# Splitting the last store of an MLP kernel over two queues and widening the zero constant of its opening matmuls

## The chip, the cores and the metric

The kernel runs on one core of one Trainium2 chip. The metric is the device time of one execution in microseconds; before the change it is 124.99 us, the median of three runs (124.86 to 125.08). Engines are named as in the profile: PE multiplies matrices (PEld is its loading of weights), DVE and ACT copy or transform tiles, POOL does small fills, SP only issues transfers. Transfers (DMAs) are issued by SP and by ACT, each on a queue of its own, and are carried out by 16 DMA engines that both queues share.

## The reference

```python
h = jnp.einsum("bsd,df->bsf", x, w1)      # x: 1 x 2048 x 640, w1: 640 x 1728
h = _silu(h)
out = jnp.einsum("bsf,fd->bsd", h, w2)    # w2: 1728 x 640, out: 1 x 2048 x 640
```

Everything is bf16 in memory: two matrix products with a SiLU between them.

## The kernel before

**Staging.** `x` comes in transposed by the DMA (`xT`, model dimension on the partitions), `w1` and `w2` lie in `w1s`, `w2s` and, for the last 64 rows of `w2`, `w2t`. The first product makes `hT`, the hidden dimension on the partitions, in groups of 512 tokens; ACT applies SiLU as it empties each PSUM bank. The second product makes the output. Columns 512 to 639 of the output are made transposed for 512 tokens at a time (class `Wide`), turned round by a DMA into `o_sb`; columns 0 to 511 are made token tile by token tile (class `Tok`), 128 tokens on the partitions. PSUM has eight banks of 512 columns; `bank()` hands them out in turn.

**The opening.** The program has a part that runs ahead of a barrier between the engines. `early` moves instructions into it. The order there: SP issues the transposing load of the first 512 tokens (two of the five blocks of `x`), ACT issues the first five column blocks of `w1`, DVE fills the small constant `z` with zero (line 125), and PE, as soon as `z` is filled, multiplies zero by zero: 13 dummy matmuls of 128 x 256 and then a pair of half width (lines 129 to 138). They write PSUM bank 3, which the first real matmul into it starts anew. Behind them on PE comes `opening()`: the real matmuls, which wait for the first `xT` and `w1s`. So a PE that starts its dummies later comes to its first real matmul later, unless the loads are later still. The two operands of a dummy are one column of `z`, repeated by a step of zero.

**The end.** The last four token tiles and a bit are not run in groups of four as the others, but one after the other: A, B, C (512 columns each), E (tile 15, columns 0 to 383) and G2 (tile 15, columns 384 to 511), lines 369 to 379. Each is closed by `close` (lines 314 to 325): an engine copies the bank into `o_sb`, then the tile is stored. E is copied by DVE and stored by SP; G2 is copied by ACT. Its store carries columns 384 to 639, that is G2's own 128 and the 128 turned ones: 128 rows of 512 bytes, 64 KB. It is the last store of the kernel, and the only one that ACT issues (`last` is true for it alone). At the end SP waits for all its stores and ACT for its one (lines 380 and 381):

```python
wait(sp, *stores)
wait(act, *stores_a)
```

No scheduler decides an order here: each engine's instructions stand in the order in which the code emits them, and semaphores (`wait`, `tick`) tie the engines together. Each DMA has a semaphore of its own, which rises as each of the 16 DMA engines reports.

Of the kernel before, what the change touches and what calls it, by code (L numbers as in the profile page):

```python
# [9 lines left out]
def bass_standalone__dense_activation_silu__prompt_kernel(  # L10
# [6 lines left out]
    bf16 = mybir.dt.bfloat16  # L17
# [3 lines left out]
    of = out.flatten_outer_dims()  # L21
    S, D = xf.shape
    F = w1.shape[1]
    P = 128
# [6 lines left out]
    HB = 256  # L31
# [7 lines left out]
    pe, act, dve, pool, sp = nc.tensor, nc.scalar, nc.vector, nc.gpsimd, nc.sync  # L39

    with ExitStack() as es:
        def sb(name, shape, dtype):
            return es.enter_context(nc.sbuf_tensor(name, shape, dtype))
# [7 lines left out]
        oT = sb("oT", [P, S], bf16)  # L51
        o_sb = sb("o_sb", [P, S // P, D], bf16)
        warm = sb("warm", [P, 32], fp32)
        z = sb("z", [P, 2], bf16)
        ps = es.enter_context(nc.psum_tensor("ps", [P, NB, BANK], fp32))

        count = {}
# [2 lines left out]
        def sem(name):  # L60
            s = es.enter_context(nc.semaphore(name))
            count[s.name if hasattr(s, "name") else name] = 0
            return [s, 0]

        def tick(ins, s, n=1):
            ins.then_inc(s[0], n)
            s[1] += n
            return (s, s[1])

        def wait(eng, *points):  # L70
            for pt in points:
                if pt is None:
                    continue
                s, v = pt
                key = (id(eng), id(s))
                if seen.get(key, 0) < v:
                    eng.wait_ge(s[0], v)
                    seen[key] = v
# [6 lines left out]
        def load(eng, out_ap, in_ap):  # L85
            s = sem(f"s_ld{n_dma[0]}")
            n_dma[0] += 1
            return tick(eng.dma_start(out=out_ap, in_=in_ap), s, 16)
# [40 lines left out]
        def dummies(n, w):  # L129
            for _ in range(n):  # L130
                for c0 in range(0, P, w):
                    pe.matmul(ps[c0:c0 + w, 3, 0:HB], lhsT=z[:, 0:1].broadcast_to([P, w]),  # L132
                              rhs=z[:, 0:1].broadcast_to([P, HB]), start=True, stop=True)

        def first_dummies():
            wait(pe, p_z)
            dummies(13, P)
            dummies(1, HC)
# [96 lines left out]
        for q in range(NSC // 2):  # L235
            b = bank()
            for k in range(DT):
                for hh in range(2):
# [3 lines left out]
                             start=(k == 0), stop=(k == DT - 1), shared=True)  # L242
# [4 lines left out]
        def evac(out_ap, in_ap, b, after, eng=None):  # L247
            e = eng or (dve, act)[evac_n[0] % 2]
            evac_n[0] += 1
            wait(e, after)  # L250
            if e is dve:
                r = tick(dve.tensor_copy(out=out_ap, in_=in_ap), s_dve)  # L252
            else:
                r = tick(act.copy(out=out_ap, in_=in_ap), s_act)  # L254
            bank_free[b] = r
            return r

        JB = SCH // P
        HP = P // 2
        stores, stores_a = [], []  # L260
        s_turn = [sem(f"s_turn{c}") for c in range(NSC)]
        st_w = [None] * NSC

        class Wide:
# [16 lines left out]
            def close(self, t):  # L281
                c = self.c
                r = evac(oT[:, c * SCH:(c + 1) * SCH], ps[:, self.b, :], self.b, t)
                wait(sp, r)
                st_w[c] = tick(sp.dma_start_transpose(
                    out=o_sb[:, c * JB:(c + 1) * JB, DA:D],
                    in_=oT[:, c * SCH:(c + 1) * SCH],
                ), s_turn[c], 16)

        class Tok:  # L290
# [23 lines left out]
            def close(self, t, eng=None):  # L314
                st, a, e = self.st, self.a, self.e
                r = evac(o_sb[:, st, a:e], ps[:, self.b, 0:e - a], self.b, t, eng)
                if e == DA:
                    e = D
                    last = a > 0
                else:  # L320
                    last = False
                q = act if last else sp
                wait(q, r, st_w[st // JB])
                (stores_a if last else stores).append(
                    load(q, of[st * P:(st + 1) * P, a:e], o_sb[:, st, a:e]))

        def lanes(up, down):
            for i in range(max(len(up), len(down))):
# [32 lines left out]
        last = None  # L361
        for q in range(NSC // 2):
            for j in range(0, JB, 2):
# [3 lines left out]
                else:  # L367
                    last = (s0, s1)
# [41 lines left out]
```

## Time and profile before

| | |
|---|---|
| median of three runs | 124.99 us (124.86 to 125.08) |
| profiled execution, its own time | 124.23 us |
| its span | 122.67 us |
| around the span | 1.56 us |
| PE busy | 120.2 us (98%), 1056 matmuls |
| ACT busy | 38.8 us |
| DVE busy | 6.8 us |
| last matmul starts / ACT's copy of G2 | 120.52 / 120.78 to 121.04 us |
| ACT's last store issued / landed / end of span | 121.07 / 122.63 / 122.67 us |

How to read it: the span runs from the first to the last instruction of the program on the core; a DMA issue is shown on its issuing engine as SPq or ACTq with the time that the issuing took, and the transfer itself goes on behind it. "Landing" is when the semaphore of a DMA is full. The profile is of one execution, which was 0.76 us shorter than the median of the runs, so differences are read from it and added to the median.

### The profile page before, as it was taken

To read this page: it belongs to the slowest core of one execution; us is meant where nothing else is said; L and a number is where in the kernel's file an instruction comes from. 1 tells how busy PE (TensorE), PEld (TensorE's weight loads), DVE (VectorE), ACT (ScalarE), POOL (GpSimd) and SP (SyncE) were. 2 spreads that over 40 slices of the span, in tenths; PEclk is the share of its full clock that TensorE was granted. 3 is DMA by queue.
4 is the path that set the end of the run, shared out by engine and by line. 5 is a ranking of instruction groups with operands and counts; after the bars stand their busy time and mean duration, and the time that the engine had idled before them with its cause. 6 is when DMAs were issued, how large, how long until landed. Compare 5 with 4: busy or idle time off the path is not lost.

```text
span 122.7 us, 2298 instructions
## 1 busy us (share of the span) xinstructions
PE 120.2 (98%) x1056; PEld 58.9 (48%) x1057; DVE 6.8 (6%) x11; ACT 38.8 (32%) x67; POOL 0.3 (0%) x5
## 2 busy tenths in 40 slices
PE   8999999999999999999999999999999999999993
PEld 5455545555555555555544444444444444444452
DVE  0000000000000000000000022002101200222001
ACT  0403975555555555555530011002101200110110
POOL 0000000000000000000000000000000000000000
PEclk9999999999999999999999999999999999999999
DMA  7999955455992000000000014202200220022122
GB/s 148 246 222 336 129 122 113 95 88 97 285 392 69 0 0 0 8 0 0 0 0 5 0 35 93 48 0 107 107 0 5 107 107 0 5 107 107 53 78 82
DMA packets 19481, 10.42 MB, mean 85 GB/s; under 512 B 13456, under 2 KB 18960, under 8 KB 19472
## 3 DMA queue, kind: packets, MB, share of 16 engines
q1 hardware_dynamic: 19184, 10.05, 32.0%
q10 hardware_dynamic: 288, 0.23, 0.7%
q8 instruction: 8, 0.13, 0.5%
q14 instruction: 1, 0.01, 0.0%
HBM read 4.51 MB, written 2.62 MB: 58 GB/s over the span
## 4 chain that ended last, share of the span: by engine, by line
PE 98%; issue 0%; ACT 0%; DVE 0%
PE ps L172 95%; PE ps L132 3%; ACT o_sb L254 0%; DVE z L125 0%
## 5 line engine op out<-in xcount | busy, mean ns | idle before, releaser
L172 PE MATMUL ps<-xT,w1s 128*64 128x512 bf16 x540 | 58.7, 380 | 0.0
L172 PE MATMUL ps<-w2s,hT 64*128 64x512 bf16 (+3 forms) x376 | 46.0, 369 | 0.2 <-issue 0.2
L172 PEld LDWEIGHTS ps<-xT,w1s 128*64 128x64 bf16 x540 | 30.0, 110 | 28.4 <-issue 0.2
L176 ACT ACTIVATE hT<-ps 128x512 bf16<-128x512 f32 x52 | 30.0, 607 | 24.5 <-PE ps L172 24.5
L172 PEld LDWEIGHTS ps<-w2s,hT 64*128 64x128 bf16 (+1 forms) x377 | 21.0, 95 | 24.1 <-issue 0.2
L254 ACT CAST o_sb<-ps 128x512 bf16<-128x512 f32 (+1 forms) x9 | 5.0, 551 | 41.5 <-PE ps L172 41.5
L172 PE MATMUL ps<-hT,w2s 64*128 64x512 bf16 x104 | 11.7, 376 | 0.0
L172 PEld LDWEIGHTS ps<-hT,w2s 64*128 64x128 bf16 x104 | 5.0, 94 | 6.3 <-issue 0.4
L252 DVE CAST o_sb<-ps 128x512 bf16<-128x512 f32 (+1 forms) x8 | 5.4, 675 | 40.5 <-PE ps L172 40.5
L252 DVE CAST oT<-ps 128x512 bf16<-128x512 f32 x2 | 1.4, 692 | 73.2 <-PE ps L172 73.2
L254 ACT CAST oT<-ps 128x512 bf16<-128x512 f32 x2 | 1.2, 586 | 10.6 <-PE ps L172 10.6
L132 PE MATMUL ps<-z 128*128 128x256 bf16 (+1 forms) x15 | 3.3, 419 | 0.4 <-DVE z L125 0.4
L172 PE MATMUL ps<-w2t,hTt 64*128 64x512 bf16 (+2 forms) x17 | 2.9, 363 | 0.0
L154 ACT ACT_TABLE_LOAD x1 | 1.3, 1283 | 4.7 <-DVEq L395 4.7
L132 PEld LDWEIGHTS ps<-z 128*128 128x128 bf16 (+1 forms) x15 | 1.9, 142 | 1.5 <-issue 0.4
L176 ACT ACTIVATE hTt<-ps 128x512 bf16<-128x512 f32 x2 | 1.2, 598 | 1.0 <-PE ps L172 1.0
L172 PEld LDWEIGHTS ps<-w2t,hTt 64*128 64x128 bf16 x17 | 0.9, 94 | 1.1
L172 PE MATMUL ps<-hTt,w2t 64*128 64x512 bf16 x4 | 0.8, 376 | 0.0
L172 PEld LDWEIGHTS ps<-hTt,w2t 64*128 64x128 bf16 x4 | 0.2, 94 | 0.2
L154 ACT ACTIVATE warm<-warm 128x32 f32<-128x32 f32 x1 | 0.2, 231 | 0.0
L141 POOL MEMSET warm<- 128x32 f32 x1 | 0.1, 124 | 4.3 <-POOLq L395 4.3
L395 POOL MEMSET const-bfloat16-1.0<- 128x1 bf16 x1 | 0.1, 101 | 0.0
(4 smaller groups left out, 0.4 us busy)
## 6 DMA issues: line engine op xcount, KB each, us to landing
out_dram<-o_sb SPq DMA_DIRECT2D x15, 160.0 KB, 1.8
w2s<-in_w_dram SPq DMA_DIRECT2D x1, 1120.0 KB, 6.3
w1s<-in_w_dram SPq DMA_DIRECT2D x4, 256.0 KB, 3.4
w2s<-in_w_dram SPq DMA_DIRECT2D x1, 960.0 KB, 8.5
w1s<-in_w_dram SPq DMA_DIRECT2D x1, 560.0 KB, 5.5
w1s<-in_w_dram SPq DMA_DIRECT2D x1, 320.0 KB, 4.3
xT<-in_x_dram SPq DMA_TRANSPOSE x18, 3.6
w1s<-in_w_dram ACTq DMA_DIRECT2D x1, 160.0 KB, 2.4
```

What stands on the lines that cost most here:

```text
L132: pe.matmul(ps[c0:c0 + w, 3, 0:HB], lhsT=z[:, 0:1].broadcast_to([P, w]), rhs=z[:, 0:1].broadcast_to([P, HB]), start=True, stop=True)
L141: p_warm = tick(pool.memset(warm[:, :], 0.0), s_pool)
L154: act.activation(out=warm[:, :], in_=warm[:, :], func=ACT.Silu)
L172: return pe.matmul(o, lhsT=l, rhs=r, start=start, stop=stop, skip_group_check=shared)
L176: r = tick(act.activation(out=out_ap, in_=in_ap, func=ACT.Silu), s_act)
L252: r = tick(dve.tensor_copy(out=out_ap, in_=in_ap), s_dve)
L254: r = tick(act.copy(out=out_ap, in_=in_ap), s_act)
L395: nc = _bacc.Bacc("TRN2", target_bir_lowering=False, num_devices=1)
```

## The change

Two edits. The constant `z` becomes 256 columns wide (128 x 256 bf16 instead of 128 x 2), and the dummies read it as it lies: 128 or 64 of its columns as the stationary operand and all 256 as the moving one, in place of one repeated column. Their number, shapes and places stay. And the last store goes out as two DMAs of 64 rows of 512 bytes: rows 0 to 63 on ACT's queue as before, rows 64 to 127 on SP's. SP's half stands in SP's program behind the store of E; SP waits for ACT's copy before it issues it, and waits for one more store at the end. All other stores keep their form.

```diff
-        z = sb("z", [P, 2], bf16)
+        z = sb("z", [P, HB], bf16)
...
         def dummies(n, w):
             for _ in range(n):
                 for c0 in range(0, P, w):
-                    pe.matmul(ps[c0:c0 + w, 3, 0:HB], lhsT=z[:, 0:1].broadcast_to([P, w]),
-                              rhs=z[:, 0:1].broadcast_to([P, HB]), start=True, stop=True)
+                    pe.matmul(ps[c0:c0 + w, 3, 0:HB], lhsT=z[:, 0:w], rhs=z[:, :],
+                              start=True, stop=True)
...
-                q = act if last else sp
-                wait(q, r, st_w[st // JB])
-                (stores_a if last else stores).append(
-                    load(q, of[st * P:(st + 1) * P, a:e], o_sb[:, st, a:e]))
+                lanes_q = ((act, 0, HP, stores_a), (sp, HP, P, stores)) if last else ((sp, 0, P, stores),)
+                for q, r0, r1, done in lanes_q:
+                    wait(q, r, st_w[st // JB])
+                    done.append(load(q, of[st * P + r0:st * P + r1, a:e], o_sb[r0:r1, st, a:e]))
```

`HB` is 256, `HP` is 64, `P` is 128.

## The prediction

> **What bounds the kernel now.** I read the page's chain first, then the groups and the waits at the opening, then the order of time at both ends, and last the DMAs of the end.
>
> ```profile
> PE 98%; issue 0%; ACT 0%; DVE 0%
> PE ps L172 95%; PE ps L132 3%; ACT o_sb L254 0%; DVE z L125 0%
> ```
>
> The chain runs from DVE's fill of `z` (L125) through the dummies (L132) into the real matmuls (L172), then to ACT's copy and the last store. No transfer and no other engine stands between the fill and the last matmul: what moves the fill or the dummies can move everything, and so can what moves the store. In order of time the chain reads (start, length, what):
>
> ```profile
> 0.14 0.07 DVE z L125
> 0.21 0.16 issue
> 0.38 3.31 PE ps L132 x15
> 3.68 105.70 PE ps L172 x932
> ...
> 120.78 0.27 ACT o_sb L254
> ```
>
> The 0.16 us of "issue" matters: `z` is ready at 0.21, PE takes it up at 0.37. The end, in order of time (start, length, engine, operation):
>
> ```profile
> 120.64 0.33 SPq L88 DMA_DIRECT2D out_dram<-o_sb  x1
> 120.78 0.27 ACT L254 CAST o_sb<-ps 128x128 bf16<-128x128 f32 x1 [2.25 <-PE ps L172]
> 121.07 0.35 ACTq L88 DMA_DIRECT2D out_dram<-o_sb  x1
> ```
>
> SP issues E's store, ACT copies G2 and issues the last store 0.43 us behind SP's. From there nothing computes: 0.35 us issue, 0.51 us until the first packet (121.93), packets until 122.27, landing 122.46 to 122.63 as the DMA engines report, end 122.67. The last 1.6 us are this one store. How close two issues can come on one queue is shown by two earlier pairs of stores on SP:
>
> ```profile
> 95.27 0.33 SPq L88 DMA_DIRECT2D out_dram<-o_sb  x1
> ...
> 95.65 0.43 SPq L88 DMA_DIRECT2D out_dram<-o_sb  x1
> ```
>
> ```profile
> 106.92 0.33 SPq L88 DMA_DIRECT2D out_dram<-o_sb  x1
> ...
> 107.36 0.38 SPq L88 DMA_DIRECT2D out_dram<-o_sb  x1
> ```
>
> The second issue of a pair is longer the sooner it starts, and its end comes 0.475 to 0.48 us after the end of the first in both. The same spacing stands between loads of `w1s` with 2048-byte rows early in the trace (2.42 to 2.89), so it is a time per transfer and not per byte.
>
> **The change part by part.** The profiled execution took 124.23 us, 122.67 of it span and 1.56 around it, which I leave as they are; it is 0.76 below the median, so I add the sum to 124.99.
>
> *The fill of `z`.* DVE's memset is 0.059 us for one 4-byte word per row and becomes 128 words. No wide memset of DVE is in the trace. Lower bound: free. Upper: DVE's copies give 1.05 ns per element (128x512 in 0.692, 128x384 in 0.558), so 127 more words are 0.133 us; POOL's memsets give 0.84 ns per word (0.098 for one, 0.124 for 32), or 0.107. I take DVE's own row. `z` is then ready at 0.35 instead of 0.21; PE took the first `xT` 0.04 after it landed, so it would start at 0.39 instead of 0.37: +0.02. The cover is PE's own late start; without it the whole 0.133 would count, for the dummies and the real matmuls follow on each other: the first real weights load at 3.46, `xT` having landed at 3.41, and the first real matmul comes at 3.47, just as the last dummies make way. A gain is excluded, as a longer fill does not start PE sooner. Sum +0.02, between 0 and +0.13.
>
> *The dummies' operands.* 15 matmuls and 15 weight loads stay. The 128-wide dummies come every 0.213 us for 256 columns; the first real matmuls, which read columns that lie side by side, come 0.426 apart for 512 at that stage: the same per column, so the repeated column cost nothing and the wide constant gains nothing. The weight loads (0.15) lie under the matmuls. Zero; a slower read would show in the real rows and does not.
>
> *ACT's half.* It keeps its place, behind ACT's copy, at 121.07. A 64-row store is not in the trace (the two 64-row loads stand in a backlog). Stores of 128 rows take 0.33 to issue whether a row has 768 or 1280 bytes, so I take 0.354, this store's own row. Bound below: half of it, -0.18.
>
> *SP's half.* One wait for ACT's copy (E's store left 0.03 after DVE's copy, ACT's 0.03 after ACT's own), one issue, one semaphore at the end. SP is through with E's issue at 120.97, so it is free at 121.08, and both halves are asked for within 0.01 us. Behind them on SP stand only the final waits. Before, SP passed those already fulfilled between 121.02 and 121.43; 0.41 us from a half issued as late as 121.9 is 122.3, ahead of any landing. Hidden; it would show only if that walk took twice as long. SP passed E's landing in 0.044 us, ACT its last in 0.038: +0.01.
>
> *The two halves together* decide it. No two stores start together in the trace, so I bound it. At best both are made ready side by side, and the 16 DMA engines share the same 128 rows: each moved 8 rows at 0.023 us, and now moves 4 and 4, plus a second completion packet of 0.009. At worst the second waits for the first as on one queue. The nearest row across queues is the last store itself: it took 0.354, where SP alone takes 0.332, and ended 0.456 after E's store, close to the 0.475 of one queue. The other ACT issue (0.12, 0.38) fell into an SP transposing issue; it was longer still, and that SP issue took 1.33 where its twin at 5.12, also of two blocks, took 1.24. Two out of two such meetings show a stretch; I take it that the halves are made ready one after the other. Against it: ACT's first load moved its first packets at 1.13, before SP's issue around it ended, so a long transposing issue does not shut the other queue out as a whole.
>
> Then: first half's issue ends 121.426, the second 0.456 later, 121.88. Issue end to last landing was 1.205; 4 rows fewer behind it are -0.093, so 1.112: landing at 122.99 against 122.63, +0.36. With 0.01 for the wait and 0.02 for the fill, +0.39: **125.38**. Ends: half the spacing for half the rows leaves about +0.1; 0.475 and a bare 0.133 of fill give +0.52.
>
> [...]
>
> **The rivals.** *Side by side, no gain.* SP's half, 0.44 after E's store like the row at 107.36, is issued in 0.38, to 121.46, 0.03 behind ACT's; the DMA engines do the same work, +0.01; with 0.01 and 0.02 +0.07: 125.06. For it: an engine's 8 rows set the time from first packet to report. Against it: the two stretched issues. [...]
>
> *Faster.* If the readying goes by rows and each queue has its own, the 0.86 us from issue to first packet shrinks. Halving the issue alone is -0.18, the whole 0.86 is -0.43; the DMA engines' starts, now spread over 0.15, come -0.07 closer. With the fill that is -0.23 to -0.48, 124.76 to 124.51; it counts as faster once more than some 60% of the 0.86 goes by rows. Against it: 0.83 to the first packet at 1280 bytes as at 768, and five times as many descriptors (the 128x5x256 load) kept the 0.476 spacing. For it: no row has fewer than 128 rows without a backlog.
>
> *The wide fill on the path.* If PE were ready earlier in most executions than in the profiled one, +0.13 in place of +0.02, with either case: 125.17 with the halves side by side, still within the bound.
>
> **How the numbers follow.** 0.2%, about what a measurement of this kernel can tell from no change, is 0.25 us: 124.74 and 125.24. One after the other 0.45, of which the half spacing (within the bound) 0.03; side by side 0.41, of which 0.02 slower through the fill and small delays at SP; faster 0.14, of which the issue alone, within the bound, 0.03. So slower 0.44, same 0.45, faster 0.11. Slower and same are nearly even: "same" gathers pieces of three cases, while the likeliest single course is one after the other, whose time I give; its own range is 125.25 to 125.51. The range of all reaches down to the faster case's upper end, 124.76, and up to 125.51.
>
> **What would show it.** In the changed profile: ACT's half at about 121.09 and SP's within 0.02 of it; one of them about 0.8 long, or its first packets 0.45 behind the other's, if they go one after the other; both below 0.4 and landing together if side by side. Landings before 122.5 would be the faster case. The fill should read about 0.19, the first dummy 0.39, and the dummies' spacing should stay 0.213. The prediction is wrong if the two issues overlap in full, or if a 64-row DMA is made ready in clearly less time than a 128-row one.

## The result and the profile after

The changed kernel takes 125.23 us against 124.97, medians of 22 runs each; the ratio is 1.0029 with a 95% interval of 1.0015 to 1.0043, that is 0.36 us slower (0.19 to 0.54). The runs of one kernel spread over 1.1 to 1.3 us, so the interval, not a single run, carries this. The profiled execution of the changed kernel took 124.87 us, its span 123.4.

The page's chain, by engine and by line, has kept its shape (where it named the fill of `z` before, it now names DVE's sequencer, DVEq L395, over the same stretch):

```profile
PE 98%; issue 0%; ACT 0%; DVEq 0%
PE ps L172 95%; PE ps L132 3%; ACT o_sb L254 0%; DVEq L395 0%
```

The same chain in order of time (start, length, what):

```profile
0.15 0.19 DVEq L395
0.34 0.05 issue
0.39 3.31 PE ps L132 x14
3.69 105.86 PE ps L172 x976
...
120.96 0.27 ACT o_sb L254
```

At the opening the longer fill has eaten most of the "issue" that stood between it and PE (0.16 us before, 0.05 now), and the first dummy starts at 0.39 instead of 0.38. The fill itself, in order of time:

```profile
0.16 0.17 DVE L125 MEMSET z<- 128x128 uint32 x1 [0.16 <-issue]
```

At the end, in order of time (SP's two issues are merged into one line; the stretch from 121.2 alone shows the second):

```profile
120.96 0.27 ACT L254 CAST o_sb<-ps 128x128 bf16<-128x128 f32 x1 [2.25 <-PE ps L172]
121.25 0.55 ACTq L88 DMA_DIRECT2D out_dram<-o_sb  x1
```

```profile
121.25 0.52 SPq L88 DMA_DIRECT2D out_dram<-o_sb  x1
```

Both halves were asked for within 0.004 us, and both issues are far longer than the 0.35 of the one store that they replace. The DMA view of the stretch from 121.0 to 123.4, a column for every 0.06 us, shows what follows:

```profile
DMA  0000000000069997300000014751257410000000
GB/s 0 0 0 0 0 0 0 0 0 0 13 218 333 371 371 231 90 13 0 0 0 0 0 34 119 196 146 43 77 162 188 103 26 0 0 0 0 0 0 0
...
out_dram<-o_sb SPq DMA_DIRECT2D x1, 32.0 KB, 1.8
out_dram<-o_sb ACTq DMA_DIRECT2D x1, 32.0 KB, 2.1
```

The first hump is E's store. Then come two humps, SP's half and behind it ACT's, whose first packets are 0.27 us apart, with the DMA engines at most seven tenths busy in a slice of either. The last lines, of issues, give the landings: ACT's half lands 2.1 us after its issue began, where the whole store took 1.6.

From the end of ACT's copy to the last landing it is 2.124 us; before it was 1.589. So the end has grown by **0.535 us**, which the interval of the times (0.19 to 0.54) only just holds; why the times show less, 0.36, stays open. The spans of the two profiled executions differ by 0.71; the other 0.18 lies in the opening, as the last matmul starts at 120.70 instead of 120.52. There PE's weight loads waited 0.7 us in all for parts of `w1s`, 0.2 before. One execution of each can't put this down to the change: with the same constant, below, the last matmul starts earlier than in the profile of before.

### The profile page after: what moved, and what is told of

It is laid out like the page before. It is cut to its first block, busy times and chain, and to the rows that moved or that the text cites. A ratio compares the mean times of both kernels' runs of the same rounds, so it can differ in the third digit from the quotient of the medians.

```text
span 123.4 us, 2300 instructions
## 1 busy us (share of the span) xinstructions
PE 120.4 (98%) x1056; PEld 59.5 (48%) x1057; DVE 6.9 (6%) x11; ACT 38.8 (31%) x67; POOL 0.3 (0%) x5
## 4 chain that ended last, share of the span: by engine, by line
PE 98%; issue 0%; ACT 0%; DVEq 0%
PE ps L172 95%; PE ps L132 3%; ACT o_sb L254 0%; DVEq L395 0%
## 5 line engine op out<-in xcount | busy, mean ns | idle before, releaser
L172 PEld LDWEIGHTS ps<-xT,w1s 128*64 128x64 bf16 x540 | 30.5, 110 | 28.0 <-DMA w1s<-in_w_dram 0.7
```

The costliest lines, as they stand in the source:

```text
L172: return pe.matmul(o, lhsT=l, rhs=r, start=start, stop=stop, skip_group_check=shared)
```

## The experiments

All lengths at the end below count from the end of ACT's last copy to the last landing, in the profiled execution, unless they are said to count from an issue. First packets and landings are read from the trace's records of single DMA packets and semaphore events. Every length is from one execution, and the kernels that store only part of the rows, and the one with both halves on ACT's queue, ran once.

**The split alone.** The constant and the dummies are those of before.

```diff
-        z = sb("z", [P, HB], bf16)
+        z = sb("z", [P, 2], bf16)
...
-                    pe.matmul(ps[c0:c0 + w, 3, 0:HB], lhsT=z[:, 0:w], rhs=z[:, :],
-                              start=True, stop=True)
+                    pe.matmul(ps[c0:c0 + w, 3, 0:HB], lhsT=z[:, 0:1].broadcast_to([P, w]),
+                              rhs=z[:, 0:1].broadcast_to([P, HB]), start=True, stop=True)
```

> The split alone, with the narrow constant and the repeated column of before. Theory (the split carries the whole loss): the two issues, asked for within 0.01 us, read about 0.52 and 0.55 us as in the changed kernel, SP's packets come about 0.27 us before ACT's, and from the end of ACT's copy to the last landing it takes 2.1 us (1.58 before, 2.115 in the changed kernel); the time is 0.3 to 0.5 us above before, ratio 1.0024 to 1.0043. Rival (the fill of the constant carries part): the end is as long, but the ratio is at most 1.0015, the rest being the fill.

125.00 us against 124.45, ratio 1.0054 (1.0029 to 1.0079), so 0.67 us (0.36 to 0.98). The operations on the output (least/median/greatest length in ns; SP's greatest is its half, the last that it issues):

```profile
L88 SPq DMA_DIRECT2D out_dram<-o_sb x17: 332/333/521, 83.6 to 121.1; - x17
L88 ACTq DMA_DIRECT2D out_dram<-o_sb x1: 551/551/551, 121.1 to 121.1; - x1
```

The issues are 0.521 and 0.551, the two queues' first packets 0.27 apart, the end 2.127: the changed kernel's end to 0.003 us. The ratio is above the expected band, though its interval holds the 0.54 us of the end. The split carries the loss.

**The wide constant alone.** Only the first of the two edits, with the one store of before.

> The wide constant alone, with the one store of before. Theory (the late start of PE and the late first load cover the fill): the fill takes 0.165 us instead of 0.059, the first dummy starts 0.01 to 0.02 us later, from the end of ACT's copy to the last landing it takes 1.58 us; the time is within 0.15 us of before. Rival (the fill stands on the path in most executions): 0.10 to 0.13 us above before. [...]

124.44 us against 124.45, ratio 1.0014 (0.9984 to 1.0044). The fill:

```profile
0.17 0.17 DVE L125 MEMSET z<- 128x128 uint32 x1 [0.17 <-issue]
...
0.39 0.39 PE L132 MATMUL ps<-z 128*128 128x256 bf16 x1 [0.39 <-DVE z L125]
```

The first dummy starts 0.016 us later than before, the dummies keep their 0.213 spacing, the end is 1.581. In this execution the last matmul starts at 120.32, 0.20 earlier than in the profile of before, in the changed kernel 0.18 later, with the same constant: the opening differs from execution to execution by more than the fill can be worth. The times bound the fill only loosely; that it costs 0.01 to 0.02 us rests on the profile. Nor do they exclude a gain by the wide operand, for the interval reaches 0.2 us below before. The traces give it little support: the first two pairs of real matmuls are 0.22 us apart here and 0.32 in the changed kernel, mostly 0.43 with the narrow constant, but 0.24 with it too in two executions below (96 and 32 rows; 48 rows).

**One half alone.** ACT stores rows 0 to 63, and SP's half is gone.

```diff
-                lanes_q = ((act, 0, HP, stores_a), (sp, HP, P, stores)) if last else ((sp, 0, P, stores),)
+                lanes_q = ((act, 0, HP, stores_a),) if last else ((sp, 0, P, stores),)
```

> As the split alone, but SP's half is left out: rows 64 to 127 of the last store are not written, so its time holds only ACT's 64 rows. Theory (the loss comes from two issues meeting): alone, the 64-row store is issued in 0.33 to 0.38 us, its first packet comes 0.83 to 0.86 us after the issue starts, and the last landing 1.45 to 1.6 us after the end of ACT's copy. Rival (a 64-row store is slow in itself): issue 0.50 us or more, first packet 1.1 us or more after its start, landing 1.85 us or more after the copy.

No other half is under way here, and yet (the same view):

```profile
L88 ACTq DMA_DIRECT2D out_dram<-o_sb x1: 532/532/532, 121.5 to 121.5; - x1
```

against, before, for twice the rows:

```profile
L88 ACTq DMA_DIRECT2D out_dram<-o_sb x1: 354/354/354, 121.1 to 121.1; - x1
```

First packet 1.19 us after the issue began (0.86 for 128 rows), landing 1.841 after it (1.559). The end is 1.871. My theory fell: half of the loss, 0.28 of 0.535 us, is the 64-row store itself, with half the bytes and no other issue beside it.

**Both halves on ACT.** In the change's line, `(sp, HP, P, stores)` becomes `(act, HP, P, stores_a)`.

> As the split alone, but both halves go out on ACT's queue, one behind the other. [...] Rival (the loss is between the queues, and one queue does not suffer it): second half less than 0.3 us behind the first, last landing 1.75 us or less after the copy. Second rival (64-row transfers are slow in themselves): each issue 0.5 us or more, landing beyond 2.3 us.

```profile
L88 ACTq DMA_DIRECT2D out_dram<-o_sb x2: 531/570/610, 121.6 to 122.1; - x2
```

The first half is as slow as alone (0.531), the second takes 0.610 and ends 0.639 after the first; the end is 2.514. The second rival holds. One behind the other on one queue costs 0.64 us for the second, on two queues 0.25: the two queues do overlap most of the readying, but not all.

**Pieces by columns.** Both queues store 128 rows of 256 bytes at the same time.

```diff
-                lanes_q = ((act, 0, HP, stores_a), (sp, HP, P, stores)) if last else ((sp, 0, P, stores),)
+                lanes_q = ((act, 0, P, stores_a), (sp, 0, P, stores)) if last else ((sp, 0, P, stores),)
...
+                    a0, a1 = (a, e) if not last else ((a, DA) if q is act else (DA, e))
-                    done.append(load(q, of[st * P + r0:st * P + r1, a:e], o_sb[r0:r1, st, a:e]))
+                    done.append(load(q, of[st * P + r0:st * P + r1, a0:a1], o_sb[r0:r1, st, a0:a1]))
```

> The last store in two by columns instead of rows: 128 rows of 256 bytes on ACT's queue (columns 384 to 511) and 128 rows of 256 bytes on SP's (columns 512 to 639), asked for at the same time; constant as before. Theory (two losses: 64 rows cost 0.28 us in themselves, and two transfers are made ready one behind the other, 0.25 us): only the second is left; the issues read 0.33 to 0.40, the two queues' first packets are 0.2 to 0.5 us apart, the last landing is 1.75 to 2.0 us after the end of ACT's copy. Rival (the whole loss comes from 64 rows): both queues' packets overlap, last landing at most 1.65 us after the copy and the time as before within 0.15 us.

```profile
L88 ACTq DMA_DIRECT2D out_dram<-o_sb x1: 367/367/367, 121.1 to 121.1; - x1
```

SP's issue, behind E's on the same queue:

```profile
121.14 0.38 SPq L88 DMA_DIRECT2D out_dram<-o_sb  x1
```

It took 0.376 and ended 0.475 after E's, the spacing that pairs on SP's queue had before; so its length is no sign of a wait for ACT. ACT's issue is 0.013 longer than for the one store. First packets are 0.07 us apart, SP's piece lands at 1.580, ACT's at 1.744. The end is just under the theory's band and above the rival's, and the packets overlap more than the theory said. ACT's piece lands 0.155 us later than the one store did: its first packet comes 0.08 later, from its last packet to its landing it takes 0.10 longer, and its packets are through 0.03 sooner. The time is as before, 0.9998 (0.9969 to 1.0026). Without the 64 rows most of the loss is gone.

**Other counts of rows, one store alone.** ACT stores the first 96, 32 or 48 rows, or the middle 64 (32 to 95), by the bounds in the same line.

> One store of rows 0 to 95 on ACT's queue; rows 96 to 127 are not written, so its time holds only three quarters of the last store. One 64-row store alone took 0.53 to issue, 1.19 to its first packet and 1.84 to its landing; 128 rows took 0.35, 0.86 and 1.56. Theory (every row count but 128 takes a slower way): about 0.5 to 0.6, 1.15 to 1.3, 1.8 to 2.0. Rival (time falls with the rows that are more, or 96 is like 128): issue below 0.4 and landing below 1.65.

> One store of rows 0 to 31 on ACT's queue; rows 32 to 127 are not written, so its time holds only a quarter of the last store. Theory (a slower way for every row count but 128): issue 0.45 to 0.6 us, first packet 1.1 us or more after the issue, landing 1.75 us or more after it. Rival (the slowness is that of 64 rows alone, 32 being like 128 but shorter): issue below 0.36, landing below 1.5.

> One store of rows 0 to 47 on ACT's queue; rows 48 to 127 are not written, so its time holds three eighths of the last store. 32, 96 and 128 rows took 0.35 to 0.36 to issue, 64 rows 0.53. Theory (64 stands alone): 0.36, landing 1.44 to 1.52 us after the issue. Rival (a band of row counts around 64 is slow): issue above 0.45, landing above 1.7.

> One store of 64 rows from the middle, rows 32 to 95, on ACT's queue; the other 64 rows are not written, so its time holds half of the last store. Theory (it is the count of 64 rows): as with rows 0 to 63, issue about 0.53, first packet 1.19 and landing 1.84 us after the issue. Rival (it is the place, one end of the partitions): issue 0.36 or less, landing 1.55 or less.

| rows stored | issue | first packet after the issue began | landing after the issue began |
|---|---|---|---|
| 32 (0 to 31) | 0.357 | 0.865 | 1.426 |
| 48 (0 to 47) | 0.356 | 0.864 | 1.439 |
| 64 (0 to 63) | 0.532 | 1.191 | 1.841 |
| 64 (32 to 95) | 0.586 | 1.246 | 1.835 |
| 96 (0 to 95) | 0.358 | 0.867 | 1.535 |
| 128 (before) | 0.354 | 0.860 | 1.559 |

The same view of the operations on the output, first for 96 rows, then for the middle 64:

```profile
L88 ACTq DMA_DIRECT2D out_dram<-o_sb x1: 358/358/358, 121.5 to 121.5; - x1
```

```profile
L88 ACTq DMA_DIRECT2D out_dram<-o_sb x1: 586/586/586, 122.2 to 122.2; - x1
```

My theory that every count but 128 goes a slower way fell with 96 and 32 rows. Of the five counts it is 64 alone, at either place and, in the changed kernel, on either queue; all with rows of 512 bytes. The rows' own price is small: from 32 to 128 the landing grows by 0.13 us. Why 64 is slow no run here shows.

**96 and 32 rows.** The split as in the change, over both queues, with other bounds.

```diff
-                lanes_q = ((act, 0, HP, stores_a), (sp, HP, P, stores)) if last else ((sp, 0, P, stores),)
+                lanes_q = ((act, 0, 96, stores_a), (sp, 96, P, stores)) if last else ((sp, 0, P, stores),)
```

> The last store in two by rows over the two queues as in the change, but 96 rows on ACT and 32 on SP instead of 64 and 64; constant as before. Theory (64 rows are slow in themselves, 32 and 96 are not; what is left is the meeting of two queues): issues of 0.35 to 0.40, last landing 1.60 to 1.78 us after the end of ACT's copy instead of 2.12, time 0.0 to 0.2 us above before. Rival (any two pieces by rows that meet suffer as the halves did): landing 1.95 us or more after the copy, time 0.35 us or more above before.

```profile
L88 ACTq DMA_DIRECT2D out_dram<-o_sb x1: 379/379/379, 121.5 to 121.5; - x1
```

SP's issue took 0.376 again, 0.474 behind E's; ACT's is 0.021 longer than for 96 rows alone. The end is 1.666 us, 0.46 shorter than with 64 and 64, at the same bytes and on the same two queues. It is still 0.08 longer than one store, and the time is 124.96 against 124.76, ratio 1.0021 (1.0000 to 1.0042). A cut by rows gains nothing even where the count is a fast one.

**Less in the last store.** The turned columns of the last tile, ready long before, go out earlier on SP; ACT's last store keeps G2's 128 columns.

```diff
                 if e == DA:
-                    e = D
                     last = a > 0
+                    e = DA if last else D
...
+        wait(sp, st_w[G2.st // JB])
+        stores.append(load(sp, of[G2.st * P:(G2.st + 1) * P, DA:D], o_sb[:, G2.st, DA:D]))
         for u, eng in ((A, dve), (B, act), (C, act), (E, dve), (G2, act)):
```

> A version meant to beat both: the 128 turned columns of the last token tile (512 to 639), which lie ready long before, go out earlier as a store of their own on SP, and the last store on ACT carries only G2's 128 columns, 128 rows of 256 bytes; constant as before. Theory (packet time grows with bytes, 23 ns at 512, 33 at 768, 54 at 1280, so about 13 at 256): 8 rows per DMA engine save 0.08 us, last landing 1.48 to 1.54 us after the end of ACT's copy, time 0.03 to 0.12 us below before, which the times can hardly tell. Rival (rows of 256 bytes to memory cost more than their bytes): last landing 1.6 us or more after the copy, time 0.05 us or more above before.

The end is 1.513 us, 0.076 shorter than before, as worked out from the packets. The time is 124.70 against 124.83, ratio 0.9985 (0.9959 to 1.0011): the gain is shown in the profile, and the times can't tell it from nothing. It is the one way found here in which the end gets shorter.

## Why the prediction came out as it did

The forecast was 125.38, +0.39 us; measured is +0.36 (0.19 to 0.54) by the ratio, 125.23 by the median. The direction and about the size are right, and at the place that was named, the last store. The working under it is right only in part, for two terms were off, in opposite ways, and that the number came so near is partly luck: for the end itself 0.37 was forecast and 0.535 came, while the times show less than the end does.

- *The fill*: forecast 0.19 long and PE 0.02 later; measured 0.165 and 0.011 to 0.016. Right, and the cover is the one named, PE's late start.
- *The dummies' operands*: forecast zero; the spacing stayed 0.213. Right.
- *ACT's half costs what 128 rows cost* (0.354, issue alone): the step that failed. I took the 0.33 of 128 rows, the same at 768 as at 1280 bytes, for a price per transfer whatever its rows. The bytes indeed don't matter in these runs (128 rows take 0.354 on ACT's queue at 256 bytes as at 512, 0.332 on SP's at 768 as at 1280), nor do 32, 48 or 96 rows (0.356 to 0.358), but 64 rows take 0.53, and the first packet comes 0.33 later. With the shorter packet time already in it, this is +0.28 us at the end; I had put it at -0.09. The two 64-row loads in the trace of before would have been the row to look at; they stood in a backlog (0.563 and 0.946 to issue, beside 0.580 and 0.563 of the loads of 128 rows ahead of them), so they could not show it.
- *One after the other, 0.456 apart*: a delay of the second half is there, with a size of a little over half. SP's half keeps the pace of a lone one (first packet 1.17 after its issue began, landing 1.84); ACT's first packet comes 0.27 behind SP's and 0.25 later than that of ACT's lone half, and that 0.25 is what the meeting costs. The issues themselves overlap in full, from 121.247 to 121.767 and from 121.251 to 121.803, and ACT's is only 0.02 longer than alone. That the two issues overlap in full is what I had put down as a sign of being wrong: issues held one behind the other are not what happened. What I read from the last store's 0.354 beside 0.332, a wait of ACT behind SP, is not shown either way: ACT's issue takes 0.354 to 0.358 with 32, 48, 96 and 128 rows, but in all these runs E's issue ended 0.10 us before it, and none has ACT's issue without that.

Meeting SP's, ACT's issue grows by 0.01 to 0.02, and it is the first packets that stand apart, by 0.07 with two pieces of 128 rows and 0.27 with 64. Something keeps the second half's packets back after its issue; what it is no run here shows.

- *The rival "side by side"*, +0.07: closest to the pieces by columns and to 96 and 32 rows (ends +0.155 and +0.08), not to the change itself. The DMA engines that both halves go over do not explain the 0.535: they were at most seven tenths busy in a slice of 0.06 us, and 96 and 32 rows, the same bytes over the same engines, cost 0.08.
- *The rival "faster"*, by a readying that goes by rows: the table speaks against it, as the first packet comes after 0.86 us at 32 rows as at 128.
- *SP's walk through its waits*: hidden as said; it passed the fulfilled ones by 122.22, and ACT's half landed at 123.35.

Of what I said would show it, neither an issue about 0.8 long (my estimate, from 0.354 and 0.456) nor first packets 0.45 apart came, nor were both issues below 0.4; the profile showed a third thing, both issues above 0.5.

## What to carry to other kernels

The transfer that ended this kernel is mostly a fixed time: of 1.56 us from issue to landing the rows' own share was about 0.13 when they went from 32 to 128. Cutting it in two did not divide that fixed time: in no piece did the first packet come sooner than 0.86 us after its issue began, and over two queues the later piece landed 0.08 to 0.54 us after the one store would have. What shortened the end, by 0.076 us in one profiled execution, was fewer bytes in the last store, by sending early what is ready early. Before a size is taken from a neighbouring row of the profile, ask whether that very shape is in the trace: here one count of rows out of five was the exception, and a single store of it, with nothing else changed, showed that at once.

## What the runs showed of the hardware that was not expected

- A lone store of 64 rows of 512 bytes on ACT's queue is issued in 0.53 to 0.59 us and lands 1.84 us after its issue began; 32, 48, 96 and 128 rows take 0.354 to 0.358 and 1.43 to 1.56.
- Rows of 256 bytes in the last store did not cost more than rows of 512: 128 of them landed 1.483 us after the issue began, 128 of 512 bytes 1.559.
- The opening varies by more than either edit is worth: the last matmul starts between 120.32 and 121.68 us in the thirteen profiled executions, whose openings differ in the constant alone. All of that arises in the first 27 us, for from the 201st real matmul on record to the last each execution takes 95.16 to 95.19. In the profile of before the first two pairs of real matmuls are 0.426 us apart and from 4.2 us on the spacing is 0.216; in the execution with the turned columns early, whose opening has the same instructions, the first pairs come at 3.88 and stay 0.426 apart until 5.6:

```profile
3.88 1.92 PE L172 MATMUL ps<-xT,w1s 128*64 128x512 bf16 x8 [0.20 <-DMA xT<-in_x_dram]
```

Eight matmuls, four pairs, in 1.92 us. This and the wait for loads, both in the opening, are what spreads the executions over more than 1 us, as far as the profiled ones show.
